# RWKV-7 attention and a SwiGLU block on one core: products with the triangular inverse as 64-row blocks, and a new step order

## The chip, the core and the metric

The kernel is one program on one core of a Trainium2 chip. The core has five engines that take their own instruction streams in order: TensorE (PE; its weight loads are listed apart as PEld), VectorE (DVE), ScalarE (ACT), GpSimd (POOL) and SyncE (SP), which issues DMAs. The metric is the device time of one execution in microseconds, the median over several runs. The profile shows one more execution, on whose trace all readings rest.

## What is computed

Two blocks stand one behind the other. The first is a recurrence over 768 time steps for 4 batches of 8 heads with 40 channels each; its state is a 40x40 matrix for each of the 32 heads:

```python
for t in range(S):
    y[:, :, t] = np.einsum('bhd,bhde->bhe', rt, state)
    Sa = np.einsum('bhde,bhe->bhd', state, at)
    state_decay = state * wt[:, :, None, :] - np.einsum('bhd,bhe->bhde', Sa, bt)
    state = state_decay + np.einsum('bhd,bhe->bhde', vt, kt)
```

Its output, 3072 tokens of 320 numbers, is the input x of the second block:

```python
xn = x / np.sqrt(np.mean(x * x, axis=-1, keepdims=True) + 1e-06) * rms_g
g = xn @ w_gate                       # 320 x 1536
out = (g / (1 + np.exp(-g)) * (xn @ w_val)) @ w_out
```

The four weights of the second block arrive as 64-bit floats and are narrowed to 32 bits on the chip. All else is in 32-bit floats.

## The kernel before, in words

**Chunks.** Time is cut into 24 chunks of 32 steps (C = 32, NCH = 24). Inside a chunk the recurrence is solved in closed form: the products of a and b (and of a and k) across the steps of a chunk form a 32x32 triangular matrix for each head, its inverse gives the vectors Sa of all 32 steps at once, and from these come the chunk's outputs and the state that it hands on. All 32 heads go together: the index n (8 values) and i (2 values) name the heads' places, o the two halves of partitions.

**front(c)** (lines 705 to 811) loads chunk c, turns it on TensorE, and builds at five levels (1, 2, 4, 8, 16 steps) the scaled copies K, A, the running products T of the decay w, and from each level's product on TensorE ("gramk") the entries of the triangular matrix in tile LT and the keys KN of that level. At the last level (l = 16) the final A becomes aP (for the product with the old state), and the last K, turned once more ("turnS"), becomes KN32 (for the update of the state). Then four DMAs carry LT to DRAM (sB) and four carry it back in another layout (M).

**inverse(c)** (lines 813 to 846) inverts the 32 matrices on VectorE, with 31 elimination steps in Yi and tmp (for the first five chunks, c < BLOCKED, only two 16x16 halves), and sends the result through DRAM (sY) by four DMAs back into LT, over the rows of the other half (line 846).

**main(c)** (lines 850 to 983) does the chunk: "state" and "lower" put the right-hand side into the PSUM tile X; line 865 copies it to Xs with a minus sign; "solve" (line 867) multiplies by the inverse from LT, 32 calls of mm() with 32 rows and 32 columns of weights, into U; for c < BLOCKED a correction with tile LB and a second solve follow (lines 870 to 877); four copies put U into VU (line 879); "update" (line 882) adds the chunk to the state with KN32, and line 886 adds the old state times its decay, Sdec (line 863). Then come the turns of r, VU and the state, "score" (line 909), its masked copies As, the products "level" and "y0", the norm of the tokens (x, with one power on POOL, line 972) and the turned copy xg for the second block.

**feed(g)** (lines 985 to 1016) is the second block for one or two chunks (groups of 1, 11 times 2, 1): products "h64" and "hh" of the weights wf with xg into PSUM, SiLU on ScalarE (sg), a product on VectorE (hT), and "out" into the PSUM tile po. Then o is copied and written by four DMAs.

**narrow** (lines 1019 to 1039) turns a slice of the 64-bit weights into 32 bits, on VectorE and ScalarE; 24 such slices lie in the early part of the run.

**The order.** None of this is issued where it is written. Every call of an operation adds a step to a list with its engine, and two strings of numbers, written out ahead, fix all: each word of ORDER names the next step to issue, counted from the first that is still open; each digit of PAIRS says which of three pairs of PSUM banks a "room" (a PSUM tile for a short time) gets. Each engine's queue gets its steps in that order. There are 6003 steps and 497 rooms. The recurrence runs two chunks ahead: in program order main(c) and its feed are followed by front(c + 2) and inverse(c + 2).

The functions pe, mm and flip wrap TensorE: mm is one product (its weights first, then what is streamed), flip one transpose. The weights' and the result's partitions fix the part of the 128x128 array that is used. by_q (line 667) lists the heads so that four neighbours lie in the four 32-row strips:

```python
half = lambda i: slice(i * 64, (i + 1) * 64)
rows = lambda i, x: slice(i * 64 + x * C, i * 64 + (x + 1) * C)
by_q = [(4 * q + m, i, o) for m in range(4) for o in range(2) for q in range(2) for i in range(2)]
other = lambda i, n: rows(i, 1 - n // 4)
```

Of the kernel before, what the change touches and what calls it, by code (L numbers as in the profile page):

```python
# [16 lines left out]
P = 128  # L17
C = 32
# [387 lines left out]
def kernel(  # L406
# [298 lines left out]
    def front(c):  # L705
# [59 lines left out]
        for j, l in list(enumerate(LEVELS))[2:]:  # L765
# [11 lines left out]

            t = Tl[l].rearrange("p n (g x) -> p n g x", x=2)
            K1 = K_.next()
            if G == 1:  # L780
                tt(K1[:, :, :, 0:16], K[:, :, :, 0:16], t[:, :, None, :, 1].to_broadcast((P, NI, 2, 16)), MUL)
            else:
                for x in range(2):
# [316 lines left out]
```

## Time and profile before

| what | value |
|---|---|
| median of 3 runs | 1028.57 us (1028.31, 1028.57, 1038.66) |
| profiled execution | 1039.87 us, of which the span from first to last instruction is 1038.0 |
| mean granted TensorE clock in it | 0.952 |
| TensorE busy | 934.5 us in 24592 matmuls |
| VectorE busy | 790.2 us in 2747 instructions |
| ScalarE, GpSimd busy | 498.4 us, 306.6 us |
| moved by DMA | 68.89 MB, most of it in packets under 512 B |

A busy share is the time in which an engine worked at something. Matmuls are pipelined, so a piece of TensorE work is best read from its start to the start of the piece behind it. In a group's name, out<-in stands for the tiles written and read, then come rows*columns of the weights and the shape that is streamed: ps<-Xs,LT 32*32 32x40 is the solve, ps<-VU,LT the product "lower", ps<-VU,KN the update, ps<-rE,vut the score, ps<-A,K and ps<-Ab,K the gramk products, ps<-As,KN the levels, ps<-xg,wf and po<-wf,hT the feed. Each mm() leaves two matmul records, each flip one.

### The profile page before, as it was taken

The numbers are of one execution on the slowest core, as the hardware profiler recorded it, in microseconds if no ns is written. First come the engines' busy times: TensorE is split into PE (matmuls) and PEld (weight loads), VectorE is DVE, ScalarE is ACT, GpSimd is POOL, SyncE is SP. The second block draws the span as 40 slices with busy tenths as digits, with TensorE's granted clock in tenths as the row PEclk, the third lists the DMA queues.
The fourth block names the chain that finished last, engine by engine and source line by source line (L and its number), as shares of the span: only waits on it lengthen the run. The fifth ranks groups of instructions, "written<-read, shape, count | busy, mean of one in ns | idle before, by whom it ended". The sixth has DMA issues, their size and how long they took to land.

```text
span 1038.0 us, 55525 instructions
## 1 busy us (share of the span) xinstructions
PE 934.5 (90%) x24592; PEld 760.3 (73%) x24592; DVE 790.2 (76%) x2747; ACT 498.4 (48%) x1113; POOL 306.6 (30%) x530
## 2 busy tenths in 40 slices
PE   2546767999999999999999999999999999999998
PEld 2445756877777878777778777777787787788777
DVE  8989978867869778868778679678697787777531
ACT  5566556453454464464454544534534635436131
POOL 9523234221432242233331324123232413400000
PEclk9957667899999999999999999999999999999999
DMA  7675443222242242232231232232322422420100
GB/s 159 145 173 120 99 93 82 56 63 54 43 84 38 47 95 43 60 79 42 59 84 28 62 75 55 55 68 36 76 45 55 81 41 65 75 44 8 43 7 21
DMA packets 147056, 68.89 MB, mean 66 GB/s; under 512 B 121088, under 2 KB 136384, under 8 KB 146816
## 3 DMA queue, kind: packets, MB, share of 16 engines
q1 hardware_dynamic: 128448, 42.37, 18.4%
q0 software_dynamic: 16192, 22.64, 11.8%
q8 instruction: 193, 3.16, 1.3%
q10 hardware_dynamic: 2176, 0.33, 0.2%
q14 instruction: 47, 0.39, 0.1%
HBM read 55.05 MB, written 10.22 MB: 63 GB/s over the span
## 4 chain that ended last, share of the span: by engine, by line
PE 70%; DVE 9%; DMA 7%; SPq 4%; issue 4%; ACT 2%; DVEq 0%; ACTq 0%
PE ps L532 50%; PE po L532 14%; PE ps L535 6%; SPq L529 4%; DVE Yi L486 2%; DMA LT<-sY 2%; DMA sY<-Yi 2%; DVE tmp L486 1%; DMA sB<-LT 1%; DVE LT L486 1%; DVE wf L486 1%; DMA M<-sB 1%; DVE K L486 1%; DVE y L486 1%; DVE As L486 0%
## 5 line engine op out<-in xcount | busy, mean ns | idle before, releaser
L532 PE MATMUL ps<-xg,wf 128*128 128x256 f32 (+3 forms) x1872 | 361.1, 375 | 1.1 <-DVE hT L486 0.9
L532 PEld LDWEIGHTS ps<-xg,wf 128*128 128x128 f32 (+1 forms) x1872 | 267.7, 190 | 49.1 <-issue 13.2
L532 PE MATMUL po<-wf,hT 128*128 128x320 f32 x576 | 179.7, 446 | 1.1 <-issue 1.1
L486 DVE TENSOR_TENSOR hT<-ps,sg 128x256 f32<-128x256 f32 (+1 forms) x156 | 59.8, 398 | 94.1 <-PE ps L532 56.0
L532 PEld LDWEIGHTS po<-wf,hT 128*128 128x128 f32 x576 | 102.9, 189 | 38.6 <-issue 4.0
L486 DVE TENSOR_TENSOR tmp<-Yi,M 128x24 f32<-128x24 f32 (+21 forms) x512 | 106.6, 208 | 17.4 <-DMA M<-sB 4.5
L486 DVE TENSOR_TENSOR Yi<-Yi,tmp 128x24 f32<-128x24 f32 (+21 forms) x512 | 106.8, 209 | 10.6
L509 ACT ACTIVATE sg<-ps 128x256 f32<-128x256 f32 (+1 forms) x156 | 54.0, 369 | 109.8 <-PE ps L532 106.8
L529 POOL DMA_DIRECT2D VU<-in_v_dram x92 | 53.9, 587 | 155.4 <-PE ps L532 134.4
L486 DVE TENSOR_TENSOR K<-K,T 128x512 f32<-128x512 f32 (+1 forms) x192 | 93.2, 501 | 4.4 <-PE ps L532 1.9
L519 POOL TENSOR_TENSOR ss<-ss,mhalf 128x1 f32<-128x1 f32 x24 | 14.3, 596 | 255.1 <-DVE ss L486 255.0
L532 PE MATMUL ps<-Ab,K 64*60 64x56 f32 (+2 forms) x4608 | 76.3, 220 | 12.7 <-issue 2.4
L532 PEld LDWEIGHTS ps<-Ab,K 64*60 64x60 f32 (+2 forms) x4608 | 69.3, 132 | 22.4 <-issue 10.1
L513 ACT COPY KN<-ps 128x640 f32<-128x640 f32 x96 | 65.8, 692 | 38.8 <-DVE LT L486 24.4
L529 POOL DMA_DIRECT2D kbn<-in_k_dram x92 | 54.1, 589 | 98.5 <-PE ps L532 98.5
L486 DVE TENSOR_TENSOR As<-ps,msi 128x256 f32<-128x256 f32 (+1 forms) x168 | 70.9, 453 | 15.5 <-PE ps L532 10.9
L529 POOL DMA_DIRECT2D kbn<-in_b_dram x92 | 54.1, 589 | 82.9 <-PE ps L532 81.3
L532 PEld LDWEIGHTS ps<-As,KN 128*40 128x40 f32 x3072 | 67.3, 128 | 11.6 <-issue 4.1
L532 PE MATMUL ps<-As,KN 128*40 128x32 f32 x3072 | 72.6, 208 | 2.4 <-DVE As L486 1.2
L513 ACT COPY K<-K 128x512 f32<-128x512 f32 x96 | 61.0, 636 | 27.1 <-PE ps L532 11.8
L486 DVE SCALAR_TENSOR_TENSOR Yi<-M,Yi 128x31 f32<-128x31 f32 (+6 forms) x228 | 44.5, 243 | 36.7 <-DMA M<-sB 20.0
L529 POOL DMA_DIRECT2D wn<-in_w_dram x92 | 51.8, 565 | 43.7 <-DVE KN L486 43.5
(131 smaller groups left out, 1503.4 us busy)
## 6 DMA issues: line engine op xcount, KB each, us to landing
M<-sB SPq DMA_DIRECT2D x96, 128.0 KB, 3.0
wan<-in_r_dram SPq DMA_DIRECT2D x24, 160.0 KB, 4.0
kbn<-in_k_dram POOLq DMA_DIRECT2D x92, 40.0 KB, 2.6
kbn<-in_b_dram POOLq DMA_DIRECT2D x92, 40.0 KB, 2.9
VU<-in_v_dram POOLq DMA_DIRECT2D x92, 40.0 KB, 2.7
wan<-in_w_dram POOLq DMA_DIRECT2D x46, 80.0 KB, 3.2
wan<-in_a_dram POOLq DMA_DIRECT2D x46, 80.0 KB, 2.8
wn<-in_w_dram POOLq DMA_DIRECT2D x92, 40.0 KB, 2.8
```

The costliest lines, as they stand in the source:

```text
L486: plan.add("DVE", time + more + each * size(o), 0.087, lambda at: [fn(at(o), *m(at))], [o], aps(*args))
L509: scalar(o, [a], lambda at: nc.scalar.activation(at(o), at(a), f, **kw), aps(acc), 0.1 if f in (AF.Square, AF.Relu) else 0.0)
L513: scalar(o, [a], lambda at: nc.scalar.copy(at(o), at(a)), extra=more)
L519: plan.add("POOL", 0.5, 0.06, lambda at: nc.gpsimd.tensor_tensor(o, a, b, op), [o], [a, b])
L529: plan.add(by, 0.6 if by == "POOL" else 0.45, 0.0, lambda at: queue.dma_start(out=o, in_=i), [o], [i], load=load, since=since)
L532: return o, lhsT, rhs, lambda at: nc.tensor.matmul(at(o), lhsT, rhs, start=start, stop=stop, skip_group_check=True), 4
L535: return o, i, ident, lambda at: nc.tensor.transpose(at(o), i, ident), 2
```

## The change

1. **A tile of their own for the inverses, from chunk 5 on.** The inverses land in LB instead of LT: rows of the one half in the even slots, rows of the other half in the odd ones, the rest zero (two blanks on POOL, one for each of the two LB tiles, in front(5) and front(6)). Two neighbouring slots then form a 64x64 matrix with two heads' inverses as blocks on its diagonal, and "solve" takes 16 products of 64 rows and 64 weight columns instead of 32 of 32.
2. **Steps whose result nobody reads are dropped:** for chunk 0 the making of aP and of the last T; for chunk 23 the last K, the last T, the turn of K with KN32, Sdec, and the update.
3. **ORDER and PAIRS are new as a whole:** 5995 steps, 495 rooms.

```diff
@@ front(c)
         LT = z["LT"] = LT_.next()
+        if c >= BLOCKED:
+            z["LB"] = LB_.next()
+            if c < BLOCKED + 2:
+                blank(z["LB"], 0.0)
...
-            K1 = K_.next()
...
+            if G > 1 or c + 1 < NCH:
+                K1 = K_.next()
...
+            if l == 16 and c == 0:
+                K = K1
+                break
...
-            tt(Tl[2 * l], t[:, :, :, 0], t[:, :, :, 1], MUL)
+            if G > 1 or c + 1 < NCH:
+                tt(Tl[2 * l], t[:, :, :, 0], t[:, :, :, 1], MUL)
...
-        z["KN"][32] = KN_[32].next()
...
+        if c + 1 < NCH:
+            z["KN"][32] = KN_[32].next()
...
@@ inverse(c)
-            dma(LT[rows(i, 1 - q), q::2], sY[seq(i, q)].rearrange("m (s t) -> s m t", s=C), "LT")
+            dma(LT[rows(i, 1 - q), q::2] if c < BLOCKED else z["LB"][rows(i, 1 - q), 1 - q::2], sY[seq(i, q)].rearrange("m (s t) -> s m t", s=C), "LT")
@@ main(c)
-        if c > 0:
+        if 0 < c < NCH - 1:
             tt(Sdec, ST.rearrange("p n i d -> p (n i) d")[:, :, 0:D], z["T"][32].to_broadcast((P, NI, D)), MUL)
...
         solve = [mm(U[other(i, n), o, col(n % 4)], LT[other(i, n), o * N + slot(n)], Xs[other(i, n), o, col(n % 4)])
-                 for n, i, o in by_q]
-        pe("lower", solve)
+                 for n, i, o in by_q] if c < BLOCKED else \
+                [mm(U[half(i), o, col(m)], z["LB"][half(i), o * N + 2 * m:o * N + 2 * m + 2].rearrange("p n t -> p (n t)"), Xs[half(i), o, col(m)])
+                 for m in range(4) for o in range(2) for i in range(2)]
+        pe("lower" if c < BLOCKED else "solve", solve)
...
-        up = plan.room()
-        pe("update", [mm(up[part(o), i, col(slot(n))], kn(z, 32, i, n, o), VU[half(i), n, o, 0:D]) for n, i, o in each])
...
+        if c + 1 < NCH:
+            up = plan.room()
+            pe("update", [mm(up[part(o), i, col(slot(n))], kn(z, 32, i, n, o), VU[half(i), n, o, 0:D]) for n, i, o in each])
```

More of the change, by code (lines that the diff above doesn't have):

```diff
@@ L33 @@
 ORDER = """
[202 rows of a table removed]
[203 rows of a table added]
 """
 PAIRS = """
-01201210121021200021102212200010110200100201020112101002120121012212012212110202010010102012120120012002120020000011
-21210200101022100112022211110111102001222121111021211202221200012011120122122211112120211212100022010102200020101002
-20021101010001010211121111020000111210200010012212120021012112221201202122010201200001101212210212102121021020112110
-12111102101020202122221201022110100022221210101022022002020221211202011101001210222111101200200021222021210111211010
-122221012001120211200102020212021
+01201012212121200021210002221121021021211001201020202001200212021020100001021001221110112200200210100110220010221122
+02001121212120211212011110002220200120102110211202022100001012212110121101001002220202011121022111202001022121211121
+11122002021222121202120002000000020200020120122202101121110201102102121200210102012002222020011111212210202100010110
+12121121222200101122100021010202021110110102122100020010010000010110022212111012221201101110211021220000202221011002
+1122111200110220012221121202102
 """
@@ L778, in front @@
             t = Tl[l].rearrange("p n (g x) -> p n g x", x=2)
-            K1 = K_.next()
[L780 to L783, printed above, removed]
-                    tt(side(K1[:, :, x], l, 0), side(K[:, :, x], l, 0), t[:, :, :, 1, None].to_broadcast((P, NI, G, l)), MUL)
-            kn_ = lambda k: k.rearrange("p n x (g h l) -> p (n x) g h l", h=2, l=l)[:, :, :, 1]
-            copy(kn_(K1), kn_(K))
+            if G > 1 or c + 1 < NCH:
+                K1 = K_.next()
+                if G == 1:
+                    tt(K1[:, :, :, 0:16], K[:, :, :, 0:16], t[:, :, None, :, 1].to_broadcast((P, NI, 2, 16)), MUL)
+                else:
+                    for x in range(2):
+                        tt(side(K1[:, :, x], l, 0), side(K[:, :, x], l, 0), t[:, :, :, 1, None].to_broadcast((P, NI, G, l)), MUL)
+                kn_ = lambda k: k.rearrange("p n x (g h l) -> p (n x) g h l", h=2, l=l)[:, :, :, 1]
+                copy(kn_(K1), kn_(K))
+            if l == 16 and c == 0:
+                K = K1
+                break
             if l == 16:
@@ L807, in front @@
             dma(M[m * BH:(m + 1) * BH].rearrange("p b x -> p (b x)")[:, 0:C * C], sB, "M")
-        z["KN"][32] = KN_[32].next()
-        copy(z["KN"][32].rearrange("p (n o e) -> p n o e", n=N, o=2),
-             turned(K.rearrange("p (n i) x s -> p n (i x s)", i=2), ins=TOP, outs=P)[:, :, :, 0:D])
+        if c + 1 < NCH:
+            z["KN"][32] = KN_[32].next()
+            copy(z["KN"][32].rearrange("p (n o e) -> p n o e", n=N, o=2),
+                 turned(K.rearrange("p (n i) x s -> p n (i x s)", i=2), ins=TOP, outs=P)[:, :, :, 0:D])
         z["aP"] = A
@@ L880, in main @@
                              U[other(i, 4 * q), :, 0:4 * D].rearrange("p o (n d) -> p o n d", n=4), more=0.09)
-        up = plan.room()
-        pe("update", [mm(up[part(o), i, col(slot(n))], kn(z, 32, i, n, o), VU[half(i), n, o, 0:D]) for n, i, o in each])
-        if c == 0:
-            copy(ST_.next()[:, :, :, 0:D].rearrange("p n i d -> p i n d"), up[:, :, 0:N * D].rearrange("p i (n d) -> p i n d", n=N))
-        elif c + 1 < NCH:
-            tt(ST_.next()[:, :, :, 0:D].rearrange("p n i d -> p i n d"),
-               up[:, :, 0:N * D].rearrange("p i (n d) -> p i n d", n=N),
-               Sdec.rearrange("p (n i) d -> p i n d", n=N), ADD)
+        if c + 1 < NCH:
+            up = plan.room()
+            pe("update", [mm(up[part(o), i, col(slot(n))], kn(z, 32, i, n, o), VU[half(i), n, o, 0:D]) for n, i, o in each])
+            if c == 0:
+                copy(ST_.next()[:, :, :, 0:D].rearrange("p n i d -> p i n d"), up[:, :, 0:N * D].rearrange("p i (n d) -> p i n d", n=N))
+            else:
+                tt(ST_.next()[:, :, :, 0:D].rearrange("p n i d -> p i n d"),
+                   up[:, :, 0:N * D].rearrange("p i (n d) -> p i n d", n=N),
+                   Sdec.rearrange("p (n i) d -> p i n d", n=N), ADD)
         if c % 2 == 0:
```

405 rows, old and new, of the table ORDER are left out of this document.

## The prediction

> **What bounds the kernel now.** I read the page's busy shares and slices first, then busy time by stage, then TensorE's timeline of one chunk and of the end, and last its waits.
>
> ```profile
> PE 934.5 (90%) x24592; PEld 760.3 (73%) x24592; DVE 790.2 (76%) x2747; ACT 498.4 (48%) x1113; POOL 306.6 (30%) x530
> ...
> PE   2546767999999999999999999999999999999998
> ...
> DVE  8989978867869778868778679678697787777531
> ```
>
> ```profile
> 50.00:100.00 50.00, 27.30 (x1046) 24.43 (x1049) 44.82 (x127) 31.26 (x60) 17.30 (x30) 0.59 0.64 151
> ...
> 150.00:200.00 50.00, 43.02 (x1362) 38.38 (x1362) 41.68 (x132) 28.88 (x64) 16.75 (x29) 0.77 0.33 68
> ...
> 300.00:400.00 100.00, 99.51 (x2508) 79.00 (x2506) 80.18 (x308) 48.66 (x110) 31.01 (x55) 1.00 0.29 60
> ...
> 700.00:800.00 100.00, 95.80 (x2450) 75.69 (x2450) 78.18 (x297) 45.94 (x105) 29.43 (x50) 1.00 0.28 54
> ```
>
> The columns of the second fence are the stretch, its length, then busy us of PE, PEld, DVE, ACT and POOL, and the granted clock. Two kernels stand one behind the other. Up to about 200 us VectorE is busy 83 to 92% of the time (42 to 46 of 50 us) and TensorE 40 to 86%, from 50 us on at a granted clock of 0.59 to 0.77. From there TensorE has 95 to 99.5 of every 100 us: a piece of TensorE work that is made shorter or longer moves the end by as much, unless it stood waiting anyway. Work of the other engines counts there only where TensorE waits for it.
>
> In TensorE's timeline (start, length, group, count), one chunk's three 32-row products, two pieces with 64x64 weights, and the last pieces:
>
> ```profile
> 540.28 0.79 PE L532 MATMUL ps<-ST,aP 64*32 64x40 f32 x64
> 541.00 0.79 PE L532 MATMUL ps<-VU,LT 32*32 32x40 f32 x64
> 541.72 1.34 PE L532 MATMUL po<-wf,hT 128*128 128x320 f32 x4
> ```
>
> ```profile
> 507.42 1.11 PE L532 MATMUL ps<-rE,vut 64*64 64x32 f32 x64
> 508.46 1.88 PE L532 MATMUL po<-wf,hT 128*128 128x320 f32 x6
> ```
>
> ```profile
> 520.00 1.16 PE L532 MATMUL ps<-A,K 64*64 64x56 f32 x64
> 521.08 0.48 PE L532 MATMUL ps<-xg,wf 128*128 128x256 f32 x1
> ```
>
> ```profile
> 993.38 0.79 PE L532 MATMUL ps<-Xs,LT 32*32 32x40 f32 x64
> ...
> 1002.30 2.65 PE L532 MATMUL ps<-As,KN 128*40 128x32 f32 x128
> 1004.78 0.79 PE L532 MATMUL ps<-As,kbn 128*40 128x32 f32 x32
> 1005.49 1.99 PE L532 MATMUL ps<-xg,wf 128*128 128x256 f32 x8
> ...
> 1032.90 0.83 PE L532 MATMUL ps<-VU,KN 64*40 64x40 f32 x64
> ```
>
> A piece's cost is the step from its start to the next one's. The solve (ps<-Xs,LT) that nothing holds up takes 993.38 to 994.09, where the next piece begins: 0.71 us for 64 records (each mm() in fp32 leaves two). 64 records with 64-column weights take 1.04 (rE,vut) or 1.08 us (A,K).
>
> **The sum's base.** The profiled execution took 1039.87 us (span 1038.0), 11.3 above the median 1028.57 of the three shown; one of these took 1038.66. Terms come from this trace; the sum goes onto the median, since none of them lies where only such an execution is longer.
>
> **Part 1, the solve, 19 chunks.** 32 mm() of 32 rows become 16 of 64 rows: 32 records instead of 64. The old ones use four diagonal 32x32 squares of the array, 16 records each. The new ones use only two diagonal 64x64 squares (top rows to top columns, bottom to bottom), again 16 records each. What paces such a stream? In rE,vut and A,K the starts come in bursts of four, one for each 64x64 square, about 7 ns apart, and the bursts 57 to 59 ns apart, for 32 as for 56 streamed columns: (1.04 - 0.13)/16 = 57 ns, where 0.13 is the exit, from the last record's start to a piece of another shape. So the square paces itself by its 64 weight columns. With 32 columns the round is (0.71 - 0.13)/16 = 36 ns. Sixteen rounds of 57 ns take as long with two squares busy as with four: I take rE,vut's 1.04 (32 streamed columns, the nearest row in weights), so +0.33 us, times 19 = +6.3. Bounds: if records share one loading path, 32 of them take half of 0.91, 0.46 + 0.13 = 0.59, which is -0.12 x 19 = -2.3; if only their number counts, 32 x 9 ns + 0.13 = 0.42, -0.29 x 19 = -5.5; if load and stream of a square don't overlap, a round is 57 + 34 ns (40 columns at the 0.84 ns of a 256-column record's 216 ns step), 1.59 us, +0.88 x 19 = +16.7. I take +6.3 because the burst pattern is that of independent squares. What follows the solve (the VU copies, update, score) comes 0.33 later; hidden by the feed pieces that TensorE does next (in 17 of 19 chunks of the new list).
> The Trainium skill, TensorE: Matmul & The Clock Gate, section "Wait — 56ns, not 53.3ns?", says that matmul starts never come closer than about 25 ns. Here 64 records start in 0.58 us, 9 ns apart, so the trace does not agree. By that floor 32 records fewer would save 0.8 us a chunk, 15 in all, and the sum would be near 1011.
>
> **Part 2, where the inverse lands.** The same four DMAs of 32 KB (LT<-sY, 2.5 us to landing) go to LB instead of LT; SP issues as many. LB's last reader is the solve two chunks earlier, so no new wait: nothing. Two blanks are added on POOL, 0.66 us each (the LT MEMSETs took 0.54 and 0.79), among steps of old times 160 to 178 and 223 to 231. Behind them stand wn, kbn and VU loads and the ss power. POOL has 17 of 50 us busy there and TensorE finds its loads long landed: nothing; if the second waits for chunk 4's correction (about 222 us), at most some 2 us on a queue that stood 134 us waiting for TensorE at its VU loads alone.
>
> **Part 3, dropped steps.** Chunk 23's update is TensorE's very last piece (1032.90), after the last po product and beside the output's copy and DMA, which end the span at 1038.0: nothing. Its turn of K, 969.45 to 969.95, is on TensorE's path: -0.5. Sdec (0.82 us, at 959.9), K1, KN32 and T belong to VectorE and ScalarE, busy 43 and 28 of the 60 us before 960 and 17 and 9 of the 40 after it: nothing. Chunk 0's aP product (0.42) and T product (0.2, by its nearest row of 32 columns) lie in the stretch that VectorE bounds; they are in the next term.
>
> **Part 4, the new order.** The two lists name every step, so I read off what stands before what. TensorE: 1091 pieces instead of 1093, 775 in another place but none by more than 18; changes of array shape 530 -> 521. A change costs 0.09: the As,KN records take 2.48/128 = 19.4 ns, the 32 of As,kbn with an exit 0.71, 0.09 more than 32 x 19.4. So -0.8. VectorE in the first 200 us: summed durations ahead of the last step of the inverses 0 to 4 are 0.8, 1.6, 0.3, 0.6 and 0.4 lower, ahead of feed 0's last product 2.0 lower, of feed 1's first 0.4. I take -1.0 (bounds -2.0 and 0). SP now issues one weight slice ahead of the first w/a loads: 0.45 later, while VectorE is in its setup and reaches chunk 0's first step at 10.7: nothing. Stands from 230 us on: setting each piece against the lower quarter of its kind, 33 stands over 0.25 us add up to 28.5, 8.8 of them inside eight solves (longest 1.61):
>
> ```profile
> 500.09 0.24 PE L532 MATMUL ps<-Xs,LT 32*32 32x40 f32 x2
> 501.23 0.77 PE L532 MATMUL ps<-Xs,LT 32*32 32x40 f32 x62 [0.90 <-DMA LT<-sY]
> ```
>
> TensorE work between the product that VectorE must await before the inverse's last steps and the solve was under 10.5 us in five chunks (11, 12, 16, 18, 21), all with a stand; it is so in six of the new list (7, 10, 11, 16, 17, 18). That is one stand of about 0.9 more, while other stands move about: 0, bounds -14 (half of them gone) and +10.
>
> Sum: +6.3 - 0.5 - 0.8 - 1.0 = +4.0; 1028.57 + 4.0 = 1032.6.
>
> **Rivals.**
> - Squares don't pace themselves: the solve takes 0.59 (shared path) or 0.71 (paced by the 40 streamed columns, as in the 32-row form). 1028.57 - 2.3 - 2.3 = 1024.0, or 1026.3. For it: 0.91/64 is 14 ns a record, which one shared path gives too, as no group leaves a 64x64 square idle. Against: four starts within 20 ns, then a gap. 0.22.
> - The number of records paces: 1028.57 - 2.3 - 5.5 = 1020.8. Against: 64 records take 0.71 or 1.04 by the columns alone. 0.05. (The skill's floor above belongs here, at its higher price.)
> - The new order clears stands: half of 28.5 gone, 1032.6 - 14 = 1018. For it: every list of this length has other collisions; against: the late solves are as many. 0.14.
> - Slower: the inverse lands too late. In every chunk the solve then waits for the landing; the price is up to 1.6 (chunk 13) a chunk. It decides from 6.3 us of added standing on, four solves of 1.6 more; at seven, 11.2: 1043.8. For it: six thin chunks instead of five, chunks 7, 10 and 17 lost 3 to 6 us of margin; a 64-row product needs both halves landed, where a 32-row one needs its own. Against: the first four old records needed all four landings too. 0.14.
> - Slower: load and stream of a square in series: 1032.6 + 10.4 = 1043. Against: A,K streams 24 columns more than rE,vut (20 ns) in a round only 2 ns longer. 0.03. The Trainium skill, same page, section "The mechanism", lets a weight load overlap a running matmul only in another row group, which would make this the rule; the 2 ns do not agree with it.
>
> **How the numbers follow.** Forecast 0.42: 1032.6, its own range 1027 to 1038. One per cent, about what a measurement of this kernel can tell from no change, is 1018.3 to 1038.9. Faster: two thirds of the case that clears stands, 0.09, plus 0.05 from the first two rivals with some stands cleared: 0.14. Slower: the two slower rivals 0.17 and 0.03 of the forecast's tail: 0.20. Same: 0.66. Range 1017 to 1043: below it the better half of the clearing case, above it the worse half of late inverses and an early stretch like that of the 1038.66 execution.
>
> **What would show it.** TensorE's timeline: ps<-Xs,LB 64*64 x32, step to the next piece 1.04 (forecast), 0.59 to 0.71, 0.42, or 1.6. Starts in pairs 57 ns apart. Bracketed waits of these rows on LB<-sY: more than eight long ones speak for the late inverse. Busy time by stage: TensorE saturated from about 200 us, at most 2 earlier. The last TensorE piece a po product. The forecast is wrong if TensorE's standing after 230 us differs from before by over 10 us, or the early stretch by over 5.

## The result

| kernel | median | ratio to before |
|---|---|---|
| before, beside it | 1032.3 us (1028.31 to 1038.66, 4 runs) | 1 |
| changed | 1048.55 us (1046.57 to 1053.55, 4 runs) | 1.0132 [1.0085, 1.018] |
| changed, 12 further runs | 1049.7 us, before 1039.7 | 1.0085 [1.0056, 1.0114] |

The change makes the kernel slower by about 0.9%, 8.8 us, where 4.0 us were forecast; 1048.55 lies above the range. Of the 16 us between it and 1032.6, 3.7 are the runs of before beside it, 4.8 are the step that failed (below), and the rest, 7.4, is what four runs leave open: their interval reaches from 8.8 to 18.6 us. All ratios below are to runs of before on the same chip, and 0.001 is 1.04 us.

The page of the changed kernel, the lines that answer to those shown of before:

```profile
PE 944.0 (90%) x23904; PEld 769.3 (74%) x23904; DVE 788.9 (75%) x2742; ACT 497.7 (48%) x1110; POOL 305.9 (29%) x532
...
PE   2546778999999989999999999999999999899998
...
DVE  8999888876957868868878678679678788765631
```

The work by stage, columns as before:

```profile
50.00:100.00 50.00, 28.06 (x1090) 25.12 (x1090) 47.75 (x141) 32.91 (x63) 16.68 (x26) 0.60 0.63 158
...
300.00:400.00 100.00, 94.09 (x2328) 75.56 (x2330) 77.62 (x295) 44.55 (x100) 27.22 (x47) 0.98 0.26 53
...
700.00:800.00 100.00, 95.67 (x2356) 76.50 (x2349) 75.08 (x283) 49.20 (x110) 31.23 (x53) 1.00 0.30 61
```

TensorE is nearly saturated, as before (94.1 and 95.7 of 100 us in the last two rows, against 99.5 and 95.8). It has 688 records less, but 9.5 us more of busy time. In its timeline the new solve that nothing holds up:

```profile
503.87 1.13 PE L533 MATMUL ps<-Xs,LB 64*64 64x40 f32 x32
504.93 1.99 PE L533 MATMUL ps<-xg,wf 128*128 128x256 f32 x8
```

Its step is 1.06 us, against 0.71 before and 1.04 forecast. Then TensorE's waits from 230 us on (what waited, for what, us in all, times, longest), first before, then the changed kernel:

```profile
PE ps L532 <- issue: 12.2, 16, 1.8
PE ps L532 <- DMA LT<-sY: 2.4, 3, 1.3
...
PE ps L535 <- issue: 1.5, 1, 1.5
PE po L532 <- issue: 1.1, 1, 1.1
```

```profile
PE ps L533 <- issue: 17.2, 16, 2.7
PE ps L533 <- DVE tmp L487: 2.1, 1, 2.1
PE ps L533 <- ACT sg L510: 1.3, 1, 1.3
PE ps L536 <- issue: 1.3, 3, 0.5
```

"issue" means that TensorE stood and the profile shows nothing that it waited for. The "issue" rows add up to 14.8 us before and 18.5 after; 2.7 of the latter are in truth a late landing, told under e2. These rows are the key to what follows.

**An account of TensorE.** To compare traces I take each piece's step at the 40% point of its kind over all runs ("dense") and call the rest "stands", from chunk 5's first product to the end:

| trace | dense, us | stands, us | "issue" rows, us |
|---|---|---|---|
| before; again | 724.1; 724.1 | 47.6; 50.9 | 14.8; 15.2 |
| changed; again | 727.9; 727.9 | 56.2; 56.8 | 18.5; 17.8 |

The dense part grows by 3.8, the stands by about 7 in these two pairs. The split hangs on how kinds are told apart; the sum of the two does not.

### The profile page after: what moved, and what is told of

It is laid out like the page before. It is cut to its first block, busy times and chain, and to the rows that moved or that the text cites. A ratio compares the mean times of both kernels' runs of the same rounds, so it can differ in the third digit from the quotient of the medians.

```text
span 1046.5 us, 54130 instructions
## 1 busy us (share of the span) xinstructions
PE 944.0 (90%) x23904; PEld 769.3 (74%) x23904; DVE 788.9 (75%) x2742; ACT 497.7 (48%) x1110; POOL 305.9 (29%) x532
## 4 chain that ended last, share of the span: by engine, by line
PE 74%; DVE 9%; DMA 6%; issue 4%; ACT 3%; SPq 2%; POOL 1%; DVEq 0%; ACTq 0%; POOLq 0%
PE ps L533 53%; PE po L533 15%; PE ps L536 6%; SPq L530 2%; DVE wf L487 1%; DVE Yi L487 1%; DMA sB<-LT 1%; DMA wf<-in_moe_w_val_dram 1%; DMA M<-sB 1%; DVE tmp L487 1%; DVE y L487 1%; DVE LT L487 1%; DVE exs L487 1%; DVE K L487 1%; DVE As L487 1%
## 5 line engine op out<-in xcount | busy, mean ns | idle before, releaser
L533 PE MATMUL po<-wf,hT 128*128 128x320 f32 x576 | 182.3, 452 | 0.0
L533 PE MATMUL ps<-Ab,K 64*60 64x56 f32 (+2 forms) x4608 | 80.2, 225 | 21.3 <-issue 7.2
L533 PEld LDWEIGHTS ps<-Ab,K 64*60 64x60 f32 (+2 forms) x4608 | 72.9, 137 | 32.4 <-issue 21.6
L487 DVE TENSOR_TENSOR K<-K,T 128x256 f32<-128x256 f32 (+1 forms) x191 | 92.7, 496 | 3.2 <-PE ps L533 1.0
L514 ACT COPY K<-K 128x512 f32<-128x512 f32 x95 | 60.2, 633 | 43.5 <-PE ps L533 17.1
```

The costliest lines, as they stand in the source:

```text
L487: plan.add("DVE", time + more + each * size(o), 0.087, lambda at: [fn(at(o), *m(at))], [o], aps(*args))
L514: scalar(o, [a], lambda at: nc.scalar.copy(at(o), at(a)), extra=more)
L533: return o, lhsT, rhs, lambda at: nc.tensor.matmul(at(o), lhsT, rhs, start=start, stop=stop, skip_group_check=True), 4
```

## The experiments

The theory at first: the 64-row solve costs its 6.3 us, and some new wait costs the rest. Rivals: a late landing of the inverse; the new order; the dropped steps; the solve's shape. The first eight kernels separate these.

**e4 and e5, before and changed again.** No edit.

> The kernel before once more, unchanged, for a second trace. Its times lie between 1028 and 1039. If the spread comes from the early stretch (to 230 us, where the granted clock was 0.50 to 0.83), the chunks' starts after 230 us keep their distances and only the offset differs; chunk 5's state product started at 261.2 us in the first trace and would start at 251 to 261. If it comes from stands later on, the offset grows along the run.

> The changed kernel once more, unchanged, with a second trace. Theory D (the late fourth landing of inverse 21 is fixed by the order and comes in every execution): TensorE stands about 3 us ahead of solve 21 in this trace too, the next eight po records take about 4.4 us instead of 2.35, and the ratio to before is 4 to 6 us above that of the kernel with the one DMA moved (1.0089), about 1.013. Rival E (an accident of that execution): no such stand, ratio about 1.009.

Measured: 0.9995 [0.9968, 1.0021] and 1.0085 [1.0056, 1.0114]. The loss is real, and smaller than in the first four runs. The second trace of before is 5.2 us longer than the first, 1.9 ahead of chunk 5 and 3.3 behind it.

**e1, the changed kernel with the old form of the solve.**

```diff
-[mm(U[half(i), o, col(m)], z["LB"][half(i), o * N + 2 * m:o * N + 2 * m + 2]..., Xs[half(i), o, col(m)]) ...]
+[mm(U[other(i, n), o, col(n % 4)], z["LB"][other(i, n), o * N + 2 * (n % 4) + 1 - n // 4], Xs[other(i, n), o, col(n % 4)]) ...]
```

> The changed kernel with its order, its tile LB and its dropped steps, but the solve of chunks 5 to 23 again as 32 products of 32 rows, read from LB. Theory A (the solve costs TensorE what its own rows show, 1.06 us instead of 0.71 a piece, 19 times): 6.5 us less than the changed kernel's 1048.5, so about 1042, ratio to before about 1.010 if before is near 1032. Rival B (the piece's length is hidden, all of the loss is the order's): the same as the changed kernel, 1048. Rival C (the 64-row solve is the whole loss, through later waits too): back at before, 1032 to 1034.

Measured: 0.9978 [0.9957, 1.0000], dense 721.6. So the order and the drops take 2.5 us of dense time from before's 724.1, and the 64-row form adds 6.3 to it (721.6 to 727.9). The whole step from e1 to e5, however, is 11 us.

**e8, the dropped steps alone; e3, the 64-row solve alone** (before's order, tile LB and its blanks).

> The kernel before with its own order and its 32-row solve from LT, but without the ten steps that nobody reads. By the prediction's terms: the turn of K in chunk 23, 0.5 us of TensorE, the rest beside other work; ratio 0.9995, within 0.998 to 1.001. If the steps of chunk 0 on VectorE count in full, 0.6 more: 0.999. That the new order with the dropped steps and a 32-row solve stood at 0.9978 would then be the order's, not the dropped steps'.

> The kernel before with its own order and no step dropped, but with the tile LB (two blanks more) and the 64-row solve from chunk 5 on. Theory A (the solve alone): 6.5 us above before, ratio 1.006, about 1039 against 1032. Rival C (the solve is the whole loss): 16 above, ratio 1.015. Rival B (order alone): as before, ratio 1.000.

Measured: e8 1.0000 [0.9970, 1.0030]; e3 1.0088 [1.0058, 1.0118], that is 9.2 us where the dense part grew by 6.2. So far the excess comes with the 64-row form, in either order.

**e2, a late landing.** In the changed kernel's trace the solve of chunk 21 starts 2.67 us late, behind the last of the inverse's four DMAs, which SyncE issued 10 us after the third. e2 moves that one step of ORDER behind the third.

```profile
893.06 2.21 SPq L530 DMA_DIRECT2D LB<-sY  x3
...
905.09 0.48 SPq L530 DMA_DIRECT2D LB<-sY  x1
```

```profile
909.84 2.02 PE L533 MATMUL ps<-Xs,LB 64*64 64x40 f32 x32 [2.67 <-issue]
```

> The changed kernel with one DMA moved: the fourth landing of inverse 21 (LB<-sY) is issued right behind the third, instead of behind four sB, four M and two output DMAs on SP. Theory A (one late landing makes TensorE stand 3.5 us at solve 21, and the halved clock behind it stretches the next pieces by 2 to 3 us): 5 to 6 us less, about 1043. Rival B (the order's loss is spread over many small stands, or the solve would have stood for something else a moment later): at most 1 us less, 1047.5.

Measured: 1.0089 [1.0061, 1.0117], no gain over e5. The late landing comes and goes without the loss: the same solve stands 0.5 us in e5's trace, and 2.57 us in that of e15 (below), the fastest run of the changed kernel. The rival falls.

**e6, the solve over four squares** (on top of e2), with eight copies of U instead of four, since each head's rows then lie in the other half:

```diff
-mm(U[half(i), o, col(m)], ...)
+mm(U[half(i ^ o), o, col(m)], ...)
```

> The changed kernel with the landing of inverse 21 moved, and the 64-row solve spread over all four 64x64 squares: the products of o = 1 take the other half's columns of the array, so that a result lands in the other half of the partitions, and the four copies to VU of a chunk become eight of half the size. Theory F (a square paces itself, 57 ns a record): 8 records a square instead of 16, the solve piece 0.57 us instead of 1.06, 19 x 0.49 = 9.3 us of TensorE work less than in the changed kernel, 2.8 less than with 32 rows; ratio 0.994 to 1.000, less what eight copies cost on ScalarE (up to 19 x 0.5 us where TensorE waits for them). Rival G (both squares of a row half share one loading path, or all records share one): the piece stays at 1.06, ratio 1.009.

Measured: 1.0070 [1.0040, 1.0100]. The piece itself in its timeline:

```profile
546.04 0.68 PE L538 MATMUL ps<-Xs,LB 64*64 64x40 f32 x32
546.64 1.34 PE L538 MATMUL po<-wf,hT 128*128 128x320 f32 x4
```

0.60 us: the same 32 records over twice the squares take 0.46 us less, so a square does pace itself. Most of the gain was taken back: TensorE now waits for the copies, in a row that is 0.2 to 0.4 us in the traces of the other kernels.

```profile
PE ps L541 <- ACT VU L519: 5.8, 11, 0.9
```

**e7, the 32 products of the old solve issued twice.**

```diff
-        pe("lower", solve)
+        pe("lower", solve if c < BLOCKED else solve + solve)
```

> The kernel before with the 32 products of the solve made twice over from chunk 5 on, the second time over the first's result: 0.59 us more TensorE work in 19 chunks, 11.3 us, at the same place as the change's 0.34. Theory H (added work at the solve costs its own length): ratio 1.011. Theory I (it costs half as much again, since ScalarE's copies and what is queued behind them come later and TensorE stands elsewhere): 17 us, ratio 1.016. Theory J (the solve's stands take it up, because TensorE waits there for ScalarE's next result anyway): under 8 us, ratio 1.007.

Measured: 1.0210 [1.0177, 1.0242], 21.8 us for 1216 records that take 9 ns each, 10.9. Work put onto TensorE's path cost twice its length, in a kernel whose data and order were those of before. Its waits:

```profile
PE ps L532 <- issue: 24.1, 24, 2.2
...
PE ps L535 <- issue: 1.9, 2, 1.4
PE po L532 <- issue: 1.7, 1, 1.7
```

27.7 us against 14.8, 12.9 more: the missing 11 us lie there, and the theory of a new wait on data falls. Where do these stands lie? Counting TensorE's records, those of over 0.25 us in before lie at 5813, 6069, 6833, 7851, 10015, 11797 and so on, nearly all at the same numbers in the other trace of that kernel, and within three records of a grid whose step is 127.3 to 127.4 records. Of the "issue" rows, 14.8 us of 14.8 lie on this grid in before, 15.9 of 18.5 in the changed kernel (the late landing is off it) and 27.6 of 27.6 in e7. Each record has a weight load, so a step of the grid is about 254.7 instructions and a few others. The page counts one DMA queue that fits, for before and changed:

```profile
q8 instruction: 193, 3.16, 1.3%
```

```profile
q8 instruction: 188, 3.08, 1.2%
```

Packets and MB: 24592 / 193 = 127.4 and 23904 / 188 = 127.1 records to a packet of 16 KB. The Trainium skill, Trainium Architecture — The Big Picture, section "The software stack", gives an instruction 64 bytes, 256 to such a packet, which agrees. The packets come one by one through the whole run.

One stand, in the changed kernel's solve of chunk 14:

```profile
585.83 0.42 PE L533 MATMUL ps<-Xs,LB 64*64 64x40 f32 x6
587.13 1.00 PE L533 MATMUL ps<-Xs,LB 64*64 64x40 f32 x26 [0.87 <-issue]
588.06 2.40 PE L533 MATMUL po<-wf,hT 128*128 128x320 f32 x4
```

All operands are there, as six records have run. The queue's packet starts at 584.82, takes 0.89 us, and TensorE goes on 2.3 us after its start. So it is elsewhere: a packet mostly starts 0.6 to 1.8 us after TensorE enters the block before, and at a stand TensorE mostly enters the new block 2.2 to 3.0 us after the packet's start. So short blocks are at risk. Of those with under 3.1 us of work, 15 of 23 end in a stand in before and 18 of 36 in the changed kernel, and most of the others had an earlier packet; 15 of 18 stands and 18 of 18 end such a block. That is less than the rule in the next expectations, by which every short block ends in a stand. The third line shows what can follow a stand: four po products take 2.40 us instead of 1.34, and the granted clock of that stretch is low:

```profile
584.00:588.00 4.00, 3.13 (x168) 2.86 (x153) 3.76 (x20) 1.63 (x6) 3.09 (x6) 1.00 0.40 76
588.00:591.40 3.40, 3.40 (x28) 2.09 (x27) 2.99 (x15) 2.36 (x5) 0.00 (x0) 0.53 0.03 7
```

The Trainium skill, TensorE: Matmul & The Clock Gate, section "HAM oscillation — how this bites in real kernels", gives as the rule no gaps of TensorE above 3.4 us. The low clock lasts about 3.4 us here, but the gap ahead of it was 0.87 us (1.81 ahead of a like stretch at 748 us in e13).

New theory: the excess is where the blocks' borders fall. Changing the number of records in 19 pieces (or anything ahead of them) moves all borders behind it into other pieces. The rival keeps the stands with the pieces and their data. They are told apart by moving the stream with nothing else changed: N small products on the identity, into columns of po that nobody reads, between TensorE's first two pieces, where it stands idle anyway.

```diff
+        nc.tensor.matmul(po_[g, 0, DM:DM + 40], ident[g, g], ident[g, 0:40], start=False, stop=False, skip_group_check=True)
...
-ORDER: <first piece of TensorE> <second piece> ...
+ORDER: <first piece of TensorE> - - - ... <second piece> ...
```

Each such product leaves two records, which the first four expectations count as one; so the moves were by 30, 154, 134 and 190 records.

**e9 (before, 30 records), e10 (changed, 154), e11 and e12 (e1's kernel, 134 and 190).**

> The kernel before, with 15 small products (32x32 by 32x40 on the identity, into columns of po that nothing reads) put into TensorE's stream between its first two pieces, where it stands idle for 10 us anyway; they move every later instruction by 30 places in the stream. Theory of blocks: in the traces nearly all of TensorE's idle time that no semaphore ends lies at every 127.3rd matmul record; with the weight loads that is 256 instructions, one 16 KB packet of queue q8 (193 packets for 24592 records). A packet starts 0.6 to 1.8 us after TensorE entered the block before, and TensorE enters the new block 2.2 to 2.9 us after that, so a block whose work takes less than about 3.1 us ends in a stand. Laid over the trace of before with its stands taken out, the grid gives 14.5 us of stands where it lies now and 20.0 us when it is moved by 15 records: +5.5 us, ratio 1.005 (1.003 to 1.008). Rival (the stands belong to the pieces and their data, not to the place in the stream): 15 products in idle time cost nothing, 1.000.

> The changed kernel with 77 such products at the same place (3.5 us idle there, about 1 to 2 us of them used). Theory of blocks: the grid's stands go from 16.7 us (mean of three traces of this instruction stream) to 12.3 us, so 4.4 us less than the changed kernel: ratio to before 1.004 where the changed kernel unmoved had 1.0085. Rival (stands of the pieces and their data): 1.0085, or a little more for the added products.

> The changed kernel with the solve as 32 products of 32 rows (as in the run that had 0.9978), with 67 such products ahead. Theory of blocks: stands 20.5 us at the grid of that run, 11.6 us after a move by 67 records, the least of all places: 8.9 us less, ratio 0.989 (0.987 to 0.993), a version faster than both kernels. Rival: 0.998.

> The same with 95 products instead of 67: 28 small products more, the same work behind them. Theory of blocks: 26.9 us of stands, about the worst place: 6.4 us more than the unmoved one, ratio 1.004, and 15 us more than with 67. Rival: 0.998, the same as with 67.

Measured: e9 1.0011 [0.9986, 1.0037], e10 1.0019 [0.9995, 1.0044], e11 1.0000 [0.9961, 1.0038], e12 1.0021 [0.9994, 1.0048]. e10 lies 6.9 us under e5, with intervals that don't meet, and its "issue" rows fell from 17.8 to 11.7. So the stream's place matters for the changed kernel. In e9, e11 and e12 no move shows clear of the noise. The sums over the grid did not foretell sizes: e9 was to lose 5.5 us and e11 to gain 8.9 over e1, and neither did; but they were worked out for half of the true moves. What a place costs must be measured.

**e13 (changed, 128 records), e14 (before, 154), e15 (changed, 64), e16 (before, 64).** 128 records are one whole block: the borders fall where they fell, and only the early work is added. That work is hidden: the first gramk product behind it starts between 17.98 and 18.02 us in the changed kernel, e10, e13 and e15 alike.

> The changed kernel with 64 small products ahead. Each leaves two matmul records (the earlier runs had 30, 154, 134 and 190 where 15, 77, 67 and 95 products were put in), so these are 128 records, one block of 127.3: every later instruction lies where it lay in the blocks. Theory of blocks: as the changed kernel unmoved, 1.0085 (1.005 to 1.011). Rival (the early products by themselves took the 6.6 us away in the run with 154 records): 1.002 or so.

> The kernel before with 77 products, 154 records, as the changed kernel had where it came to 1.0019: 27 records into the next block. Theory that the work costs the same everywhere and the place adds its own stands: the two kernels differ by the priced work (3.8 us of dense time, 1.0037) give or take the stands of each at this place, 4 us; so 0.998, between 0.994 and 1.002. Rival (the loss of the changed kernel lies in its 64-row products wherever they are): 0.0085 under the changed kernel's 1.0019, so 0.9934.

> The changed kernel with 32 products, 64 records, half a block. Theory of blocks: another set of stands, so another time than 1.0085 is likely, from 1.000 to 1.011; the sums over the grid missed in the four runs before, so no nearer figure is given. Rival (stands of the pieces and their data): 1.0085.

> The kernel before with the same 32 products, 64 records. Work and place apart: 3.8 us (0.0037) under the changed kernel with 64 records, give or take 4 us of stands. Rival (the loss lies in the 64-row products wherever they are): 0.0085 under it. Theory of the pieces' data: 1.000.

| records ahead | before | changed |
|---|---|---|
| 0 | 1 | 1.0085 [1.0056, 1.0114] |
| 128, one block | | 1.0078 [1.0050, 1.0106] |
| 154 | 1.0020 [0.9997, 1.0042] | 1.0019 [0.9995, 1.0044] |
| 64 | 1.0023 [1.0004, 1.0043] | 0.9955 [0.9931, 0.9980] |

The whole block changes nothing; part of a block does. The solve of chunk 14 again, in e13 and then in e15:

```profile
594.72 0.42 PE L535 MATMUL ps<-Xs,LB 64*64 64x40 f32 x6
596.04 1.01 PE L535 MATMUL ps<-Xs,LB 64*64 64x40 f32 x26 [0.90 <-issue]
596.98 1.34 PE L535 MATMUL po<-wf,hT 128*128 128x320 f32 x4
```

```profile
578.48 1.13 PE L535 MATMUL ps<-Xs,LB 64*64 64x40 f32 x32
579.54 1.34 PE L535 MATMUL po<-wf,hT 128*128 128x320 f32 x4
```

In e13 the stand sits behind the same sixth record as in the changed kernel (its clock stayed up this time); in e15 there is none. The "issue" rows of e13, e10 and e15:

```profile
PE ps L535 <- issue: 17.4, 19, 1.8
PE ps L538 <- issue: 2.3, 4, 0.9
```

```profile
PE ps L536 <- issue: 8.8, 12, 1.5
...
PE po L536 <- issue: 1.8, 2, 1.7
PE ps L539 <- issue: 1.1, 2, 0.9
```

```profile
PE ps L535 <- issue: 10.3, 11, 2.6
PE ps L538 <- issue: 3.0, 2, 2.1
...
PE po L535 <- issue: 0.6, 1, 0.6
```

19.7, 11.7 and 13.9 us, of which 18.0, 11.7 and 10.1 lie on the grid; the stands of the account are 53.5, 47.4 and 47.4. Blocks with under 3.1 us of work are 36, 27 and 19. That the loss lies in the 64-row products wherever they are (the rival of e14 and e16) falls: at 154 records the two kernels are equal, at 64 the changed one is 0.68% faster. e15, the changed kernel with 32 products that do nothing useful, is faster than both kernels, 0.45%. Its trace ends 15 us ahead of e13's: 6 of them are stands, 9 lie ahead of chunk 5, which starts at 255.9 and 264.7 us. That start scatters between 255.9 and 265.4 among the traces of all kernels, both ends with the changed one's stream, so what the place does there stays open.

## Why the prediction was wrong, point by point

**The solve, +6.3: right.** Step 1.06 us against 1.04; dense time 6.3 us higher than in e1, 6.2 higher in e3 than in before. The square paces itself: e6's four squares bring 32 records to 0.60 us. That refutes the rivals of a shared path, of the number of records (0.59, 0.42 us a piece) and of load and stream in series (1.59). The new solve's starts come in pairs, 57 to 58 ns apart for the most part, as forecast. In e6, 32 starts in 0.60 - 0.13 us are 15 ns apart. That too is under the floor of about 25 ns of the Trainium skill, TensorE: Matmul & The Clock Gate, section "Wait — 56ns, not 53.3ns?".

**Landing in LB, at nothing: nothing speaks against it.** e3 has it with before's order; no wait on the blanks shows on TensorE.

**Dropped steps and shape changes, -0.5 and -0.8; early stretch, -1.0.** e1 holds them all: 0.9978, -2.3 us, and 2.5 us less dense time. That this is their sum to the tenth is partly luck, since e1's interval reaches from -4.5 to 0. The drops alone did not show (1.0000). The early term cannot be seen: chunk 5 starts at 261.2 us in before and 257.1 in the changed kernel, within the scatter above.

**Stands from 230 us on, "0, bounds -14 and +10": this step failed.** Measured at the changed kernel's place in the stream: 56.2, 56.8, 53.5 (e13) and 50.7 (e2), mean 54.3, against 47.6 and 50.9, mean 49.3: +5.0. With 3.8 of dense time this is 8.8, the measured 0.0085; traces of one stream differ by up to 6 us, so that close an agreement is partly luck. I took the stands for waits on data and asked what the order does to them; I had quoted one solve held by LT<-sY and counted "8.8 inside eight solves" as if all were of that kind. Most of the waits had no releaser (14.8 of 21.5 us in before), and where those lay was set by the count of instructions ahead, which the change alters by 32 records a chunk. On the grid they grew from a mean of 15.0 to one of 17.1 us in the same traces. The account's stands also hold what a low clock costs. From chunk 5 to the last 15 us of the run the granted clock is at 0.50 for 13.7, 17.1, 6.8 and 3.4 us in those four traces, against 0 and 6.8 in before's two. By the estimate that half of such time is lost, 3.4 of the +5.0 are the clock's. The bounds held the term; the point in them did not. The rival "order clears stands" was wrong in sign for this place, yet e10 and e15 show that places exist that clear about 7 us of them (47.4 against 54.3).

**Late inverse (the slower rival): wrong.** Waits that name LB<-sY are 0.5 to 1.2 us in e5, e2 and e13 (3.7 in the faster e10), against before's 2.4 for LT<-sY. Chunk 21's late landing, which stands among the "issue" rows, adds 2.7 us in the first trace, 0.5 in e5 and 0.8 in e13; e2, without it, gained nothing.

What stays open: the worth of the change apart from the place. Over the three places the changed kernel averages 1.0020 and before 1.0014; the difference, 0.6 us, is under the 3.8 of dense time, but each figure is uncertain by 2.5 us and three places are few. The count of short blocks (under 3.1 us of work) points to the place and not to the solve's form: 23 in before and 36 in the changed kernel where they stood, 25 and 27 at 154 records, 19 and 19 at 64. It is also open what starts a stretch of low clock, and so how much of it belongs to a place: one stream had 3.4 us of it in one trace and 17.1 in another. Nor is it shown what sets a packet's start to the tenth of a microsecond, which a forecast of the place would need.

## What to carry to other kernels

On a saturated engine, separate the stands that a semaphore ends from those marked "issue", and number the instructions at which the latter lie: a constant distance that matches the packets of the instruction queue points to an engine that waits for its own program, and moving the stream by part of a block tests it. Then an edit that changes the count of instructions can move the time by more than the work it was made for (7 and 13 us in the changed kernel, against 3.8; no more than 2.4 in before), so measure a change at two or three places of the stream, with a few idle instructions ahead, before it is kept or thrown away. Price an array piece by its busiest square, and ask what else must follow when the squares are spread.

## What the runs showed of the hardware that was not expected

- TensorE's program arrives during the run in packets of 16 KB, one for each 127.3 or so matmuls with their loads; a block with under 3.1 us of work can end in a stand of 0.2 to 2.2 us (15 of 23 in before, 18 of 36 in the changed kernel). From 230 us on, 14.8 us of before are stands at these borders and 27.6 of e7.
- A stand of only 0.87 us can be followed by about 3.4 us at a granted clock of 0.50 to 0.53 (588 us in the changed kernel); behind the same record in e13, one block further on, a stand of 0.90 us was not (596 us).
- 154 useless matmuls ahead took 6.9 us from the changed kernel, 64 took 13 (1.0085 to 0.9955), 128 took none that shows (1.0078).
